# A decode step on one core: the two feed-forward weights loaded behind the last keys and values, the second one in two pieces

## The chip, the core and the metric

One NeuronCore of a Trainium2 chip. The metric is device time in microseconds (us), lower is better. A time is the median of several executions; a profile is one execution, and its time axis begins at the first instruction.

Names used all through: every load of keys (K) or values (V) is 3,072 KB, except that the last head ends in three smaller pieces of 1,920, 768 and 384 KB, K0, K1, K2 and V0, V1, V2. The load before them is the last full K or V. PE is TensorE, PEld its weight loads, DVE VectorE, ACT ScalarE, SP the sync engine. A *row* is one contiguous piece that one of the 16 DMA engines moves (the prediction calls it a packet); a load *lands* when all 16 have done their rows of it. The *clock* is the share of PE's full clock that was granted; PE is *warm* at 1.00.

## The reference, cut to what matters

```python
x = A_x                                    # one token, D = 640
q = layernorm(x) @ wq                      # 32 heads of 192
p = softmax(q . k_cache * 192 ** -0.5)     # 32,768 cached positions a head
h = x + (p . v_cache) @ wo                 # 805 MB of keys and values in all
h2 = h + relu(layernorm(h) @ w1) @ w2      # w1 640 x 1536, w2 1536 x 640
```

The result is `h2`, in bfloat16. The two weights of the last line are 1,920 KB each, 0.5% of the bytes.

## The kernel before

One loop over chunks `g`; each works on a part of a K load. PE transposes blocks of K, multiplies the values of the chunk *before* (`pv(g - 1)`), then multiplies the transposed keys by the query; VectorE does the scores of the other rows. So `pv(g - 1)` stands behind the transposes of chunk `g` in PE's order.

```python
kpool, vpool = ...(bufs=3), ...(bufs=3)          # three buffers for K, three for V
for g in range(G):
    ...
    if end == 0 and c0 == 0:                     # the first chunk of K0
        load_w("w1", B_w1, kpool, "kt", [(0, P)])
        load_w("w2", B_w2, vpool, "vt", [(0, P)])
        for i in range(NEND):                    # NEND = 3
            load_k(ld + i)
        for i in range(NEND):
            load_v(ld + i)
    elif end < 0 and c0 == 0 and g > 0:
        load_k(ld); load_v(ld)
    ...
    transposes(g)
    if g > 0:
        pv(g - 1)
    scores_pe(g)
    sc = scores_dve(g)
    ...
    exp_dve(g, sc)
# ... softmax denominator, last pv, projection, layer norm
for f in range(FT):                              # h1 = relu(hn @ w1), 12 x 5 matmuls
    for c in range(DT): ...
for n in range(DT):                              # y = h1 @ w2, 5 x 12 matmuls
    for f in range(FT):
        nc.tensor.matmul(yps[:, n:n + 1], lhsT=w_t["w2", f][...], rhs=h1T[:, f:f + 1],
                         start=(f == 0), stop=(f == FT - 1))
```

All loads are issued by the sync engine (SP), in the order of the program. The weights use the K and V buffers, so a load of them waits until an older K or V has been used up.

The softmax here doesn't subtract the row's maximum and nothing guards it: scores larger than these inputs give would overflow.

## Time and profile before

| what | number | from |
|---|---|---|
| time | 1963.55 us (1963.5 to 1964.76, 4 runs) | timing |
| profiled span | 1962.3 us | page |
| sync engine's queue, share of the DMA engines | 98.5% | page |
| read from HBM | 825 MB, 420 GB/s over the span | page |
| from K0's first transpose to the end | 28.7 us | timeline |

The kernel is bound by its stream of transfers until about its last 50 us (the DMA share is 0.99 at 1905 to 1910 and 0.49 at 1912 to 1917); there the question is what the compute waits for. The view of waits for the stretch from 1905 to 1945 us (columns: us in total, times, longest us) says it in two lines:

```profile
DVE pr L265 <- DMA kt<-in_A_k_cache_dram: 15.7, 2, 11.5
PE tp L238 <- DMA kt<-in_A_k_cache_dram: 12.6, 2, 9.4
```

Each engine waits twice, for the last full K and for K0, and the longer wait, 9.4 us for PE and 11.5 for VectorE, is the one for K0. The lines of timeline, issues and DMA share for the same stretch stand in the prediction.

### The profile page before, as it was taken

Reading aid. Unit: us, or ns where it says so; the run is one execution under the profiler, and the core shown is the slowest. Engines: PE = TensorE matmul, PEld = TensorE weight load, DVE = VectorE, ACT = ScalarE, POOL = GpSimd, SP = SyncE. Lnnn points to the kernel's source line nnn. Section 1 sums busy time; section 2 is a strip of 40 time slices with the busy share of each in tenths; the row PEclk is TensorE's granted clock in tenths of the full one; section 3 lists DMA queues with packets and bytes.
Section 4 is the critical chain, followed back from the end, with each engine's and each line's share of the span. In section 5 each row is a group of like instructions: output and inputs, shape, how many; then the busy total and the mean of one; then the engine's idle time right before and its main releaser. Section 6 shows DMA issues by size and latency. Waiting matters only on the chain.

```text
span 1962.3 us, 44905 instructions
## 1 busy us (share of the span) xinstructions
PE 1588.3 (81%) x20392; PEld 1116.2 (57%) x20392; DVE 1338.0 (68%) x654; ACT 1067.8 (54%) x2223; POOL 0.7 (0%) x6
## 2 busy tenths in 40 slices
PE   5887888888878788887888788887887878787876
PEld 4555555555556556565555555555555555555554
DVE  5766776667666676776777666766766767677664
ACT  4555555555555555555555555555555545555553
POOL 0000000000000000000000000000000000000000
PEclk9988899989998998988998988988989889999997
DMA  9999999999999999999999999999999999999994
GB/s 405 430 430 431 430 427 430 429 431 430 431 430 428 431 429 430 431 428 431 430 431 430 428 431 428 432 430 423 430 428 429 427 423 430 430 430 426 430 398 187
DMA packets 51506, 827.85 MB, mean 422 GB/s; under 512 B 4596, under 2 KB 17396, under 8 KB 18548
## 3 DMA queue, kind: packets, MB, share of 16 engines
q1 hardware_dynamic: 51316, 824.99, 98.5%
q8 instruction: 159, 2.61, 0.5%
q14 instruction: 31, 0.25, 0.0%
HBM read 824.97 MB, written 0.00 MB: 420 GB/s over the span
## 4 chain that ended last, share of the span: by engine, by line
DMA 78%; PE 16%; ACT 4%; DVE 2%; issue 1%; SPq 0%; ACTq 0%
DMA kt<-in_A_k_cache_dram 78%; PE o_ps L292 7%; PE tp L238 6%; ACT kT L239 3%; DVE pr L265 1%; PE sp L248 1%; PE sp L252 1%; PE sp L250 1%; ACT pB L255 0%; PE qps L204 0%; ACT pA L275 0%; DVE o_pair L313 0%; ACT row_e L207 0%; PE den L298 0%; PE attT L336 0%
## 5 line engine op out<-in xcount | busy, mean ns | idle before, releaser
L239 ACT COPY kT<-tp 128x1024 bf16<-128x1024 bf16 (+1 forms) x1025 | 905.2, 966 | 356.2 <-PE tp L238 353.2
L265 DVE TENSOR_TENSOR pr<-kt,qb 128x2304 f32<-128x2304 bf16 (+1 forms) x258 | 655.0, 2539 | 490.7 <-DMA kt<-in_A_k_cache_dram 487.2
L238 PE MATMUL tp<-ident_b,kt 128*128 128x128 bf16 x7677 | 593.1, 241 | 359.2 <-DMA kt<-in_A_k_cache_dram 283.8
L238 PEld LDWEIGHTS <-kt 128*128 128x128 bf16 x7677 | 524.8, 109 | 398.0 <-DMA kt<-in_A_k_cache_dram 294.6
L268 DVE TENSOR_REDUCE sc<-pr 128x12 f32<-128x2304 f32 (+1 forms) x258 | 654.3, 2536 | 27.6 <-ACT kT L239 1.4
L292 PE MATMUL o_ps<-vt,pB 128*2 128x384 bf16 x2559 | 498.6, 345 | 2.6 <-DMA vt<-in_A_v_cache_dram 2.6
L292 PEld LDWEIGHTS <-pB 128*2 128x2 bf16 x2559 | 203.6, 87 | 226.5 <-issue 65.0
L255 ACT ACTIVATE pB<-sp 128x20 bf16<-128x20 f32 (+1 forms) x258 | 48.5, 188 | 489.2 <-PE sp L252 489.2
L292 PE MATMUL o_ps<-vt,pA 128*2 128x384 bf16 x1537 | 291.9, 326 | 0.0
L248 PEld LDWEIGHTS <-kT 128*128 128x128 bf16 x2559 | 196.0, 96 | 85.8 <-issue 84.4
L248 PE MATMUL sp<-qm,kT 128*128 128x2 bf16 x2559 | 218.5, 164 | 0.5 <-ACT kT L239 0.5
L250 PE MATMUL sp<-qm,kT 128*128 128x1 bf16 x2559 | 214.9, 163 | 0.0
L252 PE MATMUL sp<-qm,kT 128*128 128x1 bf16 x2559 | 214.9, 163 | 0.0
L250 PEld LDWEIGHTS <-kT 128*128 128x128 bf16 x2559 | 198.6, 96 | 0.0
L292 PEld LDWEIGHTS <-pA 128*2 128x2 bf16 x1537 | 129.2, 84 | 120.9 <-issue 0.4
L252 PEld LDWEIGHTS <-kT 128*128 128x128 bf16 x2559 | 197.4, 96 | 0.0
L275 ACT ACTIVATE pA<-sc 128x12 bf16<-128x12 f32 (+1 forms) x258 | 52.9, 205 | 0.0
L255 ACT ACTIVATION_READ_ACCUMULATOR pB<-sp 128x1 f32 x258 | 50.2, 195 | 0.0
L275 ACT ACTIVATION_READ_ACCUMULATOR pA<-sc 128x1 f32 x258 | 49.4, 191 | 0.0
L304 DVE TENSOR_REDUCE rec<-den 128x1 f32<-128x20 f32 x32 | 5.7, 179 | 62.7 <-PE den L298 62.7
L314 ACT ACTIVATE o_pair<-o_ps,rec 2x192 f32<-2x192 f32 x32 | 13.2, 412 | 26.9 <-DVE o_pair L313 26.9
L326 PE MATMUL oT_ps<-ident_f,o_pair 2*128 2x1 f32 x192 | 24.2, 247 | 0.1
(60 smaller groups left out, 192.0 us busy)
## 6 DMA issues: line engine op xcount, KB each, us to landing
kt<-in_A_k_cache_dram SPq DMA_DIRECT2D x127, 3072.0 KB, 35.7
vt<-in_A_v_cache_dram SPq DMA_DIRECT2D x127, 3072.0 KB, 31.4
wq<-in_A_wq_dram SPq DMA_DIRECT2D x8, 960.0 KB, 34.7
wo<-in_A_wo_dram SPq DMA_DIRECT2D x16, 480.0 KB, 31.5
kt<-in_B_w_dram SPq DMA_DIRECT2D x1, 1920.0 KB
vt<-in_B_w_dram SPq DMA_DIRECT2D x1, 1920.0 KB
kt<-in_A_k_cache_dram SPq DMA_DIRECT2D x1, 1920.0 KB, 28.6
vt<-in_A_v_cache_dram SPq DMA_DIRECT2D x1, 1920.0 KB, 17.6
```

The costliest lines, as they stand in the source:

```text
L238: nc.tensor.transpose(out=tp[:, b, :], in_=kt[:, off:off + P], identity=ident_b[:])
L239: nc.scalar.copy(out=kT[:, b0:b0 + nb, :], in_=tp[:, 0:nb, :])
L248: nc.tensor.matmul(sp[:, 2 * i:2 * i + 2], lhsT=kT[:, 3 * i + 1, :], rhs=qm[:, 1:3], start=True, stop=False, skip_group_check=True)
L250: nc.tensor.matmul(sp[:, 2 * i:2 * i + 1], lhsT=kT[:, 3 * i, :], rhs=qm[:, 0:1], start=False, stop=False, skip_group_check=True)
L252: nc.tensor.matmul(sp[:, 2 * i + 1:2 * i + 2], lhsT=kT[:, 3 * i + 2, :], rhs=qm[:, 3:4], start=False, stop=True, skip_group_check=True)
L255: nc.scalar.activation(out=pB[:, 0:JP], in_=sp[:, 0:JP], func=F.Exp, scale=SCALE, accum_out=dsums[:, h, 2 * c + 1:2 * c + 2])
L265: nc.vector.tensor_tensor(out=pr[:, 0:JD, :], in0=kt[:, c0 * Dh:(c0 + JD) * Dh].rearrange("p (j d) -> p j d", d=Dh), in1=qb[:].unsqueeze(1 ...
L268: nc.vector.reduce_sum(out=sc[:, 0:JD], in_=pr[:, 0:JD, :], axis=mybir.AxisListType.X)
L275: nc.scalar.activation(out=pA[:, 0:JD], in_=sc[:, 0:JD], func=F.Exp, scale=SCALE, accum_out=dsums[:, h, 2 * c:2 * c + 1])
L292: nc.tensor.matmul(o[:], lhsT=p, rhs=vt[:, (c0 + j) * Dh:(c0 + j + 2) * Dh], start=first, stop=last)
L314: nc.scalar.activation(out=dst[:, 1, n0:n0 + Dh], in_=o[:, Dh:2 * Dh], func=F.Copy, scale=s[0:2, 1:2])
L326: nc.tensor.matmul(ps[:, b:b + 1], lhsT=src[:, i, b * P:(b + 1) * P], rhs=ident_f[0:2, i:i + 1], start=(i == 0), stop=(i == 1))
```

## The change

The intent: K0 should not queue behind 3.9 MB that are needed only at the very end, and the weights should travel while the compute behind the last values runs. The second product is ordered by rows of w2, so that it could begin on the first piece.

```diff
-    def load_w(name, src, pool, tag, rows):
+    def load_w(name, src, pool, tag, pieces):
...
-        for r0, r1 in rows:
-            nc.sync.dma_start(out=v[r0:r1], in_=...[r0:r1])
+        for i in range(pieces):
+            c0, c1 = i * n // pieces, (i + 1) * n // pieces
+            nc.sync.dma_start(out=v[:, c0:c1], in_=...[:, c0:c1])
...
             if end == 0 and c0 == 0:
-                load_w("w1", B_w1, kpool, "kt", [(0, P)])
-                load_w("w2", B_w2, vpool, "vt", [(0, P)])
                 for i in range(NEND):
                     load_k(ld + i)
                 for i in range(NEND):
                     load_v(ld + i)
+                load_w("w1", B_w1, kpool, "kt", 1)
+                load_w("w2", B_w2, vpool, "vt", 2)
...
-        for n in range(DT):
-            for f in range(FT):
+        for f in range(FT):
+            for n in range(DT):
                 nc.tensor.matmul(yps[:, n:n + 1], ...,
-                                 start=(f == 0), stop=(f == FT - 1))
+                                 start=(f == 0 and n == 0), stop=(f == FT - 1 and n == DT - 1),
+                                 skip_group_check=True)
```

More of the change, by code (lines that the diff above doesn't have):

```diff
@@ L132 @@
     w_t = {}
-    def load_w(name, src, pool, tag, rows):
+    def load_w(name, src, pool, tag, pieces):
         n, N = src.shape[0] // P, src.shape[1]
-        assert n * N <= JL * Dh
+        assert n * N <= JL * Dh and n % pieces == 0
         t = pool.tile([P, JL * Dh], bf16, tag=tag, name=tag)
         v = t[:, 0:n * N].rearrange("p (c n) -> p c n", n=N)
-        for r0, r1 in rows:
-            nc.sync.dma_start(out=v[r0:r1], in_=src.rearrange("(c p) n -> p c n", p=P)[r0:r1])
+        for i in range(pieces):
+            c0, c1 = i * n // pieces, (i + 1) * n // pieces
+            nc.sync.dma_start(out=v[:, c0:c1], in_=src.rearrange("(c p) n -> p c n", p=P)[:, c0:c1])
         for c in range(n):
```

## The prediction

> **What bounds the kernel now.** I read the page first, for the row of DMA shares and the chain that ended last; then the DMA issues, the timeline and the busy time by stretch of the last 70 us. The page:
>
> ```profile
> DMA  9999999999999999999999999999999999999994
> DMA 78%; PE 16%; ACT 4%; DVE 2%; issue 1%; SPq 0%; ACTq 0%
> ```
>
> The first line is the busy share of the 16 DMA engines in 40 slices: full until the last slice (49 us). The second is the chain: 78% transfers. So for some 1,900 us the kernel streams K and V at about 430 GB/s. The change removes no byte, so that part stays. What can move is the end: work that begins only when the last keys land. The timeline of PE, then the sync engine's DMA issues (start, us, engine, line, what):
>
> ```profile
> 1918.38 1.50 PE L238 MATMUL tp<-ident_b,kt 128*128 128x128 bf16 x24
> 1920.57 1.79 PE L292 MATMUL o_ps<-vt,pB 128*2 128x384 bf16 x10
> 1922.19 1.14 PE L292 MATMUL o_ps<-vt,pA 128*2 128x384 bf16 x6
> 1933.61 2.10 PE L238 MATMUL tp<-ident_b,kt 128*128 128x128 bf16 x18 [9.45 <-DMA kt<-in_A_k_cache_dram]
> 1935.64 3.32 PE L292 MATMUL o_ps<-vt,pB 128*2 128x384 bf16 x10
> 1938.80 1.14 PE L292 MATMUL o_ps<-vt,pA 128*2 128x384 bf16 x6
> 1940.33 1.17 PE L238 MATMUL tp<-ident_b,kt 128*128 128x128 bf16 x18
> 1941.43 1.14 PE L292 MATMUL o_ps<-vt,pB 128*2 128x384 bf16 x6
> ...
> 1955.61 1.74 PE L394 MATMUL h1ps<-xn_ln,kt 128*128 128x1 bf16 x60 [1.36 <-DVE xn_ln L186]
> 1957.62 1.74 PE L401 MATMUL yps<-h1T,vt 128*128 128x1 bf16 x60 [0.27 <-ACT h1T L397]
> ```
> ```profile
> 1893.83 0.38 SPq L140 DMA_DIRECT2D kt<-in_B_w_dram  x1
> 1902.00 0.38 SPq L140 DMA_DIRECT2D vt<-in_B_w_dram  x1
> 1904.96 18.24 SPq L123 DMA_DIRECT2D kt<-in_A_k_cache_dram  x3
> 1923.25 17.53 SPq L123 DMA_DIRECT2D vt<-in_A_v_cache_dram  x3
> ```
>
> See three things. PE stands still 9.45 us for the ending keys (call the three ending pieces K0, K1, K2 and V0, V1, V2; the full-size load ahead of them is "the last full K, V"). From K0 at 1933.6 to the span's end at 1962.3 nothing waits for a transfer: it is pure compute, 28.7 us. And w1, w2 are issued ahead of K0. The busy time by stretch tells how they travel (the last two columns are DMA share and GB/s):
>
> ```profile
> 1905.00:1910.00 5.00, 3.45 (x46) 1.99 (x44) 2.52 (x1) 2.38 (x7) 0.00 (x0) 1.00 0.99 391
> 1912.00:1917.00 5.00, 5.00 (x42) 3.82 (x40) 4.86 (x3) 3.55 (x4) 0.00 (x0) 0.71 0.49 205
> 1918.00:1921.00 3.00, 2.74 (x54) 2.33 (x52) 2.90 (x2) 2.39 (x7) 0.00 (x0) 1.00 0.55 205
> 1923.00:1926.00 3.00, 1.16 (x33) 0.81 (x30) 0.00 (x0) 0.47 (x4) 0.00 (x0) 1.00 1.02 393
> 1929.00:1933.00 4.00, 0.00 (x0) 0.00 (x0) 0.00 (x0) 0.00 (x0) 0.00 (x0) 0.50 1.01 430
> 1935.00:1939.00 4.00, 4.00 (x19) 1.79 (x18) 3.86 (x3) 1.94 (x3) 0.00 (x0) 0.53 0.51 217
> ```
>
> From 1912 to 1921 and again from 1935 to 1939 the share is half. The packet records say who works: packets of 3,072 bytes (w1's rows; K2 and V2 have them too, but are not yet issued) appear from 1899 to 1905 and again from 1917 to 1922; of 1,280 bytes (w2 here) from 1904 to 1911 and again from 1922 to 1928. So one half of the engines, the leading one, runs some 18 us ahead of the other, the lagging one, and every load lands when the laggards have done their half. The laggards never rest until 1940: they end the last full V at 1917.3, w1 at 1922, w2 at 1928.3, and then reach K0. The leaders starve because K0's issue takes until 1920.
>
> **What the Trainium skill says.** "DMA: Bandwidth & Descriptors", section "Queues, rings and completion order": "On each SDMA engine descriptors are consumed in ring order". The trace agrees: K0 is 1,920 KB, 4.6 us at 430 GB/s, yet it landed 28.6 us after its issue, behind the weights. Same page, "Why a DMA increments its semaphore by 16 and not by 1": the engines of a DMA finish independently, and only the full count means that all has landed. The half shares above agree: the slower half decides. "TensorE: Matmul & The Clock Gate", "What's actually happening": after an idle window of about 3.4 us the array falls to half clock. It agrees: granted clock 0.50 at 1929 to 1933, and the 18 transposes then took 2.10 us against 1.17 for 18 warm ones. "PSUM — Partial Sum Buffer", "The four PSUM rules": two groups open at once in one bank cannot both clear the written bits; hence the changed product has one start and one stop for all five columns. No run yet shows that; the attention projection (L336) already uses this form.
>
> **The change part by part.** Instruction order: the sync engine's queue alone is reordered (one DMA more); every other engine has as many instructions as before.
>
> (a) *K0 no longer waits for w1 and w2 on the lagging engines.* K0 moves up two places in the issue order, as it now takes the key buffer that w1 took (issue near 1893.8); K1 takes the one K0 took (1905), V0 the one w2 took. On the lagging half nothing lies between the last full V (done at 1917.3) and K0. A K0 packet of 15,360 bytes took 0.573 us, 8 per engine: 4.6 us. K0 lands at about 1922.3 instead of 1933.6: 11 us earlier.
>
> (b) *PE cannot use all of it.* It ends the scores of the preceding chunk only at 1924.1. So K0's transposes start there: 1933.6 - 1924.1 = 9.5 us won, which is the whole idle time.
>
> (c) *PE stays warm.* 18 transposes: chain step 1.03 us instead of 2.10. The 16 value matmuls behind them: 2.77 us (1920.57 to 1923.33) instead of 4.3. Won: 1.07 + 1.5 = 2.5 us. The next transposes start at about 1924.1 + 1.03 + 2.8 + 0.55 (scores) = 1928.5, where they were at 1940.4.
>
> (d) *V0 may now be a little late.* Lagging half: K0 until 1922, K1 (8 x 0.234 us) 1924, K2 (8 x 0.121) 1925, V0 (4.6) 1929.6, landing about 1930. Its first matmul could start at 1929.5. Cost: 0.5 us. V1 (1931.6 on the ring) and V2 (1932.6) are wanted at 1935.6 and 1938: in time.
>
> (e) *The weights come last, behind compute.* w1: 40 packets an engine of 0.121 us, 4.8 us, until 1937.4; w2: 96 of 0.055 us, 5.3 us, pieces done at 1940 and 1942.7, landed by 1944 or so. Wanted: from the first V0 matmul to the first feed-forward product it was 1955.61 - 1941.43 = 14.1 us; from 1930.0 that makes w1's product start at 1944.1, the w2 product 2.0 us later, its second half 3 us later. w1 has 6 us to spare, w2's second piece 3 us.
>
> Their buffers: w1 takes the last full K's (read until 1920.6), w2 the last full V's (its matmuls end at 1928). Both issues come before the lagging engines are ready for them (1932.6, 1937.4).
>
> (f) *Reordering the second product*: 60 matmuls before and after, 1.75 us either way. The split in two: one more DMA. Both worth about 0.
>
> Sum: -9.5 - 2.5 + 0.5 = **-11.5 us**: span 1962.3 - 11.5 = 1950.8; the timed median is 1.2 us above the profiled span (1963.51 against 1962.3), so **1952.0 us**, 0.6% faster.
>
> **Rivals.** *Hidden anyway:* the bytes are the same and DMA is at its limit, so time stays at 1963.5. For it: 98.5% DMA share over the span. Against it: 28.7 us at the end have almost no transfers in their second half, so weights put there fill a hole. *Bytes only:* 3.93 MB at 430 GB/s is 9.1 us, so 1954.4; this misses the clock, and that the laggards take 11 us for them. *A new wait for the weights:* if the issue of w1 or w2 is held up (K0's took 15 us behind w2), or the laggards are further behind than I think, PE waits at the first or second feed-forward product; w2 landing 4 us later than in (e) would cost about 1 us, 8 us about 5, so 1953 to 1957. Against it: the K and V pieces ahead need only 8 descriptors an engine each, where w2 needs 96. *Values late:* V1 waits in the queue for a values buffer; it becomes free near 1918, well before it is needed, but if this slips by 15 us, it costs some 3 us.
>
> **Range and chances.** A gain below 9 us needs one of the last two rivals; above 13 us there is nothing left to take, since PE is then busy or in a chain of dependent steps. The runs of before lie within 1.3 us. So 1948.5 to 1957.5. A 2% change is 39 us, more than the whole tail: within 2% is nearly sure.
>
> **What would show it.** In the changed profile: no PE wait of more than 1 us for keys after 1915; K0's transposes at about 1924 at full clock; the DMA share half or full but not zero until about 1943; the h1ps matmuls at about 1944, released by xn_ln (the layer norm) and not by a DMA; the yps matmuls without a gap in their middle; the 60 yps matmuls in 1.75 us. Wrong would be a wait of PE for in_B_w ahead of h1ps or yps, or in the middle of yps (step e); a wait of the values matmuls for V1 or V2 (step d); K0 landing later than 1926 (step a).

## The result, and the profile after

The changed kernel takes **1954.31 us** (1954.08 to 1954.44, 4 runs) against 1963.55. Ratios here are the mean time of one kernel's runs over that of the other's of the same rounds, so not quite the ratio of the medians: 0.9951, 95% interval 0.9934 to 0.9969. That is 0.5% faster, within the 2% that count as the same, and 2.3 us above the predicted 1952.0. The profiled span fell by 10.0 us, to 1952.3.

The page of the changed kernel, the same two lines as before (DMA share in 40 slices; the chain that ended last):

```profile
DMA  9999999999999999999999999999999999999996
DMA 77%; PE 17%; ACT 4%; DVE 1%; issue 1%; SPq 0%; ACTq 0%
```

Only the last slice differs: the engines are busy for 0.6 of it instead of 0.4. The stream itself is as it was. Next the DMA issues of the changed kernel's sync engine:

```profile
1893.43 12.61 SPq L123 DMA_DIRECT2D kt<-in_A_k_cache_dram  x3
1906.10 13.78 SPq L123 DMA_DIRECT2D vt<-in_A_v_cache_dram  x3
1922.03 0.38 SPq L141 DMA_DIRECT2D kt<-in_B_w_dram  x1
1929.27 4.31 SPq L141 DMA_DIRECT2D vt<-in_B_w_dram  x2
```

K0 is issued at 1893.43, where w1 was; the long stretches of the first two rows are gaps between the three issues, in which the next piece waits for its buffer. Then PE (L239 transposes, L293 value matmuls, L395 and L402 the two feed-forward products):

```profile
1912.12 3.38 PE L239 MATMUL tp<-ident_b,kt 128*128 128x128 bf16 x30 [3.39 <-DMA kt<-in_A_k_cache_dram]
...
1919.74 1.50 PE L239 MATMUL tp<-ident_b,kt 128*128 128x128 bf16 x24
...
1925.38 1.16 PE L239 MATMUL tp<-ident_b,kt 128*128 128x128 bf16 x18
1926.48 1.79 PE L293 MATMUL o_ps<-vt,pB 128*2 128x384 bf16 x10
...
1929.64 1.17 PE L239 MATMUL tp<-ident_b,kt 128*128 128x128 bf16 x18
1931.56 1.14 PE L293 MATMUL o_ps<-vt,pB 128*2 128x384 bf16 x6 [0.76 <-DMA vt<-in_A_v_cache_dram]
...
1945.51 1.74 PE L395 MATMUL h1ps<-xn_ln,kt 128*128 128x1 bf16 x60 [1.36 <-DVE xn_ln L187]
1947.52 1.74 PE L402 MATMUL yps<-h1T,vt 128*128 128x1 bf16 x60 [0.27 <-ACT h1T L398]
```

K0's transposes at 1925.38 carry no wait: the 9.45 us are gone, and PE comes to them from other work. What is left is 0.76 us for V0 at 1931.56. Neither feed-forward product waits for a transfer. The first matmul on V0 moved from 1941.43 to 1931.56, by 9.9 us, and from there to the end both kernels take 20.8 to 20.9 us. The busy time by stretch in the changed kernel (last two columns: DMA share, GB/s):

```profile
1912.00:1917.00 5.00, 4.88 (x36) 3.72 (x37) 4.72 (x2) 3.55 (x4) 0.00 (x0) 0.50 0.74 316
1918.00:1921.00 3.00, 3.00 (x60) 2.37 (x58) 2.90 (x2) 1.03 (x5) 0.00 (x0) 1.00 0.69 222
1935.00:1939.00 4.00, 3.97 (x44) 2.10 (x42) 1.27 (x2) 2.47 (x7) 0.00 (x0) 1.00 0.88 321
1941.00:1944.00 3.00, 2.06 (x27) 1.87 (x27) 0.65 (x6) 1.70 (x2) 0.00 (x0) 1.00 0.38 141
```

From 1935 the engines carry the weights (0.88, then 0.38 as the leading half is done), beside PE's work on the last chunks. The column before them is the granted clock: 0.50 at 1912 to 1917, where it was 0.71 before; this was not in the prediction's account. It comes with PE's wait of 3.39 us for the last full K, but not as the idle window of about 3.4 us that the prediction quotes from the Trainium skill's page on TensorE would have it: PE stood still from 1908.73, and the trace has the clock at half from 1910.36, 1.6 us into that wait. For the 9.45 us wait of the kernel before the window does fit; for this one the measurement decides.

### The profile page after: what moved, and what is told of

Same layout as the page of the kernel before. It is cut to its first block, busy times and chain, and to the rows that moved or that the text cites. A ratio compares the mean times of both kernels' runs of the same rounds, so it can differ in the third digit from the quotient of the medians.

```text
span 1952.3 us, 44906 instructions
## 1 busy us (share of the span) xinstructions
PE 1594.4 (82%) x20392; PEld 1122.4 (57%) x20392; DVE 1338.0 (69%) x654; ACT 1067.5 (55%) x2223; POOL 0.7 (0%) x6
## 4 chain that ended last, share of the span: by engine, by line
DMA 77%; PE 17%; ACT 4%; DVE 1%; issue 1%; SPq 0%; ACTq 0%
DMA kt<-in_A_k_cache_dram 75%; PE o_ps L293 8%; PE tp L239 6%; ACT kT L240 3%; DMA vt<-in_A_v_cache_dram 1%; DVE pr L266 1%; PE sp L249 1%; PE sp L253 1%; PE sp L251 1%; PE qps L205 0%; ACT pA L276 0%; ACT pB L256 0%; DVE o_pair L314 0%; PE oT_ps L327 0%; ACT row_e L208 0%
## 5 line engine op out<-in xcount | busy, mean ns | idle before, releaser
L239 PE MATMUL tp<-ident_b,kt 128*128 128x128 bf16 x7677 | 599.3, 242 | 342.8 <-DMA kt<-in_A_k_cache_dram 269.7
L239 PEld LDWEIGHTS <-kt 128*128 128x128 bf16 x7677 | 531.1, 110 | 381.2 <-DMA kt<-in_A_k_cache_dram 280.2
L293 PE MATMUL o_ps<-vt,pB 128*2 128x384 bf16 x2559 | 498.8, 346 | 2.6 <-DMA vt<-in_A_v_cache_dram 2.6
L293 PEld LDWEIGHTS <-pB 128*2 128x2 bf16 x2559 | 203.8, 87 | 226.9 <-issue 65.9
L293 PE MATMUL o_ps<-vt,pA 128*2 128x384 bf16 x1537 | 291.9, 326 | 0.0
L293 PEld LDWEIGHTS <-pA 128*2 128x2 bf16 x1537 | 129.1, 84 | 120.8
L315 ACT ACTIVATE o_pair<-o_ps,rec 2x192 f32<-2x192 f32 x32 | 13.2, 412 | 26.9 <-DVE o_pair L314 26.9
## 6 DMA issues: line engine op xcount, KB each, us to landing
vt<-in_A_v_cache_dram SPq DMA_DIRECT2D x1, 1920.0 KB, 25.4
```

The costliest lines, as they stand in the source:

```text
L239: nc.tensor.transpose(out=tp[:, b, :], in_=kt[:, off:off + P], identity=ident_b[:])
L293: nc.tensor.matmul(o[:], lhsT=p, rhs=vt[:, (c0 + j) * Dh:(c0 + j + 2) * Dh], start=first, stop=last)
L315: nc.scalar.activation(out=dst[:, 1, n0:n0 + Dh], in_=o[:, Dh:2 * Dh], func=F.Copy, scale=s[0:2, 1:2])
```

## The experiments

Four theories were set against each other. *The lagging half* (the prediction): only the time that the slower DMA engines spend on what stands in front of K0 and V0 counts. *The split*: the pieces of w2 carry part of the gain. *The held-up issue*: the many short rows of w2 blocked K0's issue, the leading engines starved, and that was the loss. *Weights not hidden*: they cost time at the end of the changed kernel.

An interval of such a ratio is about 0.0013 to each side, 2.5 us. So differences of 1 us are read from run ranges that don't overlap and from the traces, and are called open where neither tells.

**The loads alone, and the split alone** (before: 1964.65). The first keeps the new place of the loads, with one piece and the old product order; the second keeps the old place, with two pieces and the new order.

```diff
# order_only, against the changed kernel
-                load_w("w2", B_w2, vpool, "vt", 2)
+                load_w("w2", B_w2, vpool, "vt", 1)       # and the product's loops as before
# split_only: both load_w lines ahead of load_k, the rest as changed
```

> Both weights are the last loads as in the changed kernel, but w2 in one piece and the second product in the order of before. Main theory (the position of the loads is all; the laggard half of the DMA engines reaches K0 sooner): within 0.5 us of the changed kernel, 1953.8 to 1954.8, since the last piece of w2 ended near 1944 in the changed kernel's trace and its product starts only at 1947.5. Rival (the split carries part of the gain by letting the product start on the first piece): 1955 or more, with PE waiting for in_B_w ahead of the second product.

> Weights in front of K0 as before, but w2 in two pieces and the product ordered by piece. Main theory: as before, 1963.0 to 1964.0. Rival (split or order is worth something by itself): 1 us or more below 1963.5.

Measured: the loads alone 1954.37 (ratio 0.9949), the split alone 1964.34 (0.9998, interval 0.9986 to 1.0011). The whole gain is the place of the loads. The split is worth nothing that these runs can see, as the second product wasn't waiting for w2 in any of them.

**One weight at a time**.

```diff
# w1_last: w2 ahead of load_k, w1 behind load_v.   w2_last: the other way round
```

> w2 in front of K0 (two pieces), w1 behind V2. Main theory (what counts is the time that the lagging half spends on the rows in front of K0): w2 takes 96 rows an engine of 0.055 us, 5.3 us, so K0 lands 5 us later than in the changed kernel, near 1929.5; PE, free at 1925.4, waits 4 us and may fall to half clock: 1958 to 1960.5. Rival (the loss of before came from K0's issue being held up by the many short rows of w2, which starved the leading half): almost nothing won, 1962 to 1963.5.

> w1 in front of K0, w2 behind V2. Main theory: w1 takes 40 rows an engine of 0.121 us, 4.8 us, K0 lands near 1929: 1957.5 to 1960. Rival (held-up issue by w2's short rows): with w2 away the issue runs free and nearly the whole gain is had, 1954.5 to 1955.5.

Measured: 1959.54 with only w1 moved, 1959.45 with only w2 moved: half the gain each (5.1 and 5.2 us of 10.3). K0's transposes on PE, in the run with w1 moved and then in the run with w2 moved:

```profile
1929.01 2.10 PE L239 MATMUL tp<-ident_b,kt 128*128 128x128 bf16 x18 [3.56 <-DMA kt<-in_A_k_cache_dram]
```
```profile
1929.67 2.10 PE L239 MATMUL tp<-ident_b,kt 128*128 128x128 bf16 x18 [4.53 <-DMA kt<-in_A_k_cache_dram]
```

In the changed kernel VectorE started on K0 at 1924.21, the moment it landed (PE was still busy); here K0 lands 4.8 and 5.5 us later. That each weight costs the same, though one has 40 rows an engine and the other 96, speaks for time on the engines and against the held-up issue, which asked for 1962 or more in the first run and about 1955 in the second. (The second profile is of that run's slowest execution, 1960.44 us, in which the lagging engines ended the last full V 0.7 us later than in the changed kernel.)

**All bytes in front, in long rows** (before: 1964.15). The weights are read so that a partition's row is one piece of 15,360 bytes. Its output is wrong, which doesn't matter for the time.

```diff
# and both load_w lines ahead of load_k, w2 in one piece
-            nc.sync.dma_start(out=v[:, c0:c1], in_=src.rearrange("(c p) n -> p c n", p=P)[:, c0:c1])
+            nc.sync.dma_start(out=v[:, c0:c1], in_=src.rearrange("(p c) n -> p c n", p=P)[:, c0:c1])
```

> Wrong result on purpose: weights in front of K0 with all their bytes, but read in another order, so that each partition's row is one piece of 15,360 bytes instead of 5 of 3,072 or 12 of 1,280. K0's issue then can't be held up by many rows and the leading half doesn't starve. Main theory (only the time of the lagging half counts): 16 rows of 0.573 us, 9.2 us, instead of 10.1, so about 1 us below before, which was 1964.65 on the chip of the last call: 1963 to 1964.2. Rival (held-up issue and the starved half cost time): 4 us or more below before.

Measured: 1963.37 (1962.75 to 1963.88), ratio 0.9996. Here is K0's issue before, then in this run, each from its timeline of the sync engine, and K0's transposes in this run:

```profile
1904.96 15.16 SPq L123 DMA_DIRECT2D kt<-in_A_k_cache_dram  x1
```
```profile
1905.09 0.33 SPq L123 DMA_DIRECT2D kt<-in_A_k_cache_dram  x1
```
```profile
1933.16 2.10 PE L239 MATMUL tp<-ident_b,kt 128*128 128x128 bf16 x18 [8.67 <-DMA kt<-in_A_k_cache_dram]
```

The hold-up is real: the issue took 15.16 us and now takes 0.33. But K0 lands at 1933.16 instead of 1933.61. By the packet records the leading engines had ended K0's rows at 1915.9 in this run and began them only at 1920.8 in the kernel before, and nothing came of it. This is the clearest test of the lagging half: the held-up issue falls. The Trainium skill's "Perfetto Trace Analysis", section "DMA Instruction — HWDGE (DVE, Sync)", explains how to read the 15.16 us: the profiled time of an issue is that of waiting for and using the descriptor generator, and not the data's. This agrees, since K0's own data needed about 5 us.

**Hardly any weights** (wrong result). One fifth of w1 and one twelfth of w2 in front of K0, nothing behind V2.

```diff
-        for i in range(pieces): ...
+        nc.sync.dma_start(out=v[:, 0:1], in_=src.rearrange("(c p) n -> p c n", p=P)[:, 0:1])
         for c in range(n):
-            w_t[name, c] = v[:, c, :]
+            w_t[name, c] = v[:, 0, :]
```

> Wrong result on purpose: in front of K0 only one twelfth of w2 and one fifth of w1 are loaded (557 KB instead of 3,932), and used for all products; nothing behind V2. Main theory (in the changed kernel the weights are wholly hidden, what is left is K0, V0 and a chain of compute): 8 rows of 0.121 and 8 of 0.055 us an engine, 1.4 us, stand in front of K0 and V0, so 1.0 to 1.6 us over the changed kernel, 1955.3 to 1956. Rival (the weights still cost time at the end of the changed kernel): 1954 or less, since they are nearly gone.

Measured: 1956.34 (1955.44 to 1958.0), not below the changed kernel but above it. So weights that are nearly absent gain nothing over weights loaded last: they are hidden. The time is a little above what was expected; V0 came at 1932.8 as foreseen, but after the wait of 1.95 us for it PE was at half clock for a spell (the next 15 transposes took 1.75 us instead of 1.00). The run also answers a rival that was not listed: in the changed kernel K0 is not only first in the queue but issued 11.5 us sooner (1893.43 against 1904.96). Here it was issued at 1905.10 and landed at 1925.44, so most of the gain does not need the sooner issue.

**More bytes behind V2**. Half of w2 twice more, ahead of w1 and of w2, into unused ends of their buffers.

```diff
+        x = t[:, n * N:n * N + 6 * D].rearrange("p (c n) -> p c n", n=D)
+        nc.sync.dma_start(out=x, in_=B_w2.rearrange("(c p) n -> p c n", p=P)[:, 0:6])
```

> The changed kernel with 1,920 KB more (half of w2 twice over, into unused ends of the buffers) behind V2 and ahead of w1 and of w2. Main theory: the lagging half takes 2 x 48 rows of 0.055 us, 5.3 us more, so the last piece lands near 1949.2 where it ended near 1943.9; it is wanted at 1948.4 (the middle of the second product), so 0.8 to 2 us over the changed kernel, 1955 to 1956.3, with PE waiting for in_B_w in the second product alone. Rival (no slack: the loads at the end set the end): 5 us more, 1959. Rival (slack larger than 6 us): no change.

Measured: 1955.71 (1955.3 to 1957.34). The two products on PE:

```profile
1946.50 1.74 PE L396 MATMUL h1ps<-xn_ln,kt 128*128 128x1 bf16 x60 [1.36 <-DVE xn_ln L189]
1948.51 1.90 PE L403 MATMUL yps<-h1T,vt 128*128 128x1 bf16 x60 [0.27 <-ACT h1T L399]
```

The time is within the expected range, but not for the expected reason: the second product is stretched by 0.16 us alone (1.90 against 1.74), in one gap ahead of its 31st matmul, the first on the second piece of w2. The other 1.0 us lies ahead of the first product and comes with a clock of 0.62 at 1941 to 1944. So the slack of the changed kernel is about what this load takes, some 5 us; the time itself settles nothing, as the changed kernel run again gave 1955.66.

**V0 ahead of K1 and K2**, a version to beat the changed kernel.

```diff
-                for i in range(NEND): load_k(ld + i)
-                for i in range(NEND): load_v(ld + i)
+                load_k(ld);     load_v(ld)
+                load_k(ld + 1); load_k(ld + 2)
+                load_v(ld + 1); load_v(ld + 2)
```

> The changed kernel with the last values' order K0, V0, K1, K2, V1, V2. Main theory: in the changed kernel PE waited 0.76 us for V0, behind K1 and K2 (2.9 us on the lagging half); now V0 lands before it is wanted and PE runs through: 0.5 to 1 us below the changed kernel, 1953.3 to 1954. Rival (K1 now comes late instead, or the wait moves to the buffers): no change, or slower.

Measured: 1953.20 (1951.82 to 1953.57), ratio to before 0.9943, and correct. All its runs lie below all nine timed runs of the changed kernel. They were run at other times. In its timeline the first matmul on V0 follows its transposes at once, at 1929.63, with no wait.

**The clock** (before: 1964.05). The changed kernel again, for the same rounds; then V0 early, with 50 transposes of the identity in PE's wait for the last full K; then the kernel *before*, with 140 of them in its wait for K0.

```diff
+            if end == -1 and c0 == 0:            # before_warm: end == 0, 140 times
+                wm = mm_bank([P, P], bf16, "wm")
+                for _ in range(50):
+                    nc.tensor.transpose(out=wm[:], in_=ident_b[:], identity=ident_b[:])
             transposes(g)
```

> The changed kernel itself again, to have it in the same rounds as the next ones. 1954 to 1955 with before at 1963.5 to 1964.7.

> V0 early as in the last call, and 50 transposes of the identity into an unused PSUM tile, ahead of the first transposes of the last full K, where PE stands still for 3.1 us and then works at half clock. They should take about 2.8 us (50 x 0.056) of that wait. Theory (after the last full K has landed the chain is PE's own work, and in v0_early 0.6 us of its 30 transposes and 0.9 us of the 10 value matmuls behind them come from the half clock): 1.0 to 1.6 us below v0_early, which was 1953.2: 1951.6 to 1952.3. Rival (V0 or the lagging half's next piece then becomes the wait): 0 to 0.5 us.

> The kernel before, with 140 transposes of the identity ahead of K0's transposes, so that PE works through most of its 9.45 us wait for K0 (140 x 0.056 = 7.8 us) and keeps its clock. Tests step c alone: 1.07 us of transposes and 1.5 us of value matmuls, 2 to 2.6 us below before: 1961 to 1962.5. Rival (the clock is worth nothing since something else sets the pace, the evacuations or the values): within 0.5 us of before.

Measured: changed again 1955.66 (1954.15 to 1955.71), ratio 0.9955; V0 early and warm 1952.36 (1952.18 to 1952.96), 0.9942; before and warm 1963.53 (1963.41 to 1964.13), 0.9998. The middle one is clear of the changed kernel in the same rounds, by some 3 us; that the extra transposes help beyond V0's place is not shown: it is 0.8 us across two calls, the trace has a new wait of 0.95 us for K0, and the first matmul on V0 starts at 1929.77, no sooner than the 1929.63 without them. The profile's shorter span (1950.6 against 1951.0) comes from later on, where the clock is 0.87 instead of 0.67 at 1938 to 1944. The third result was a miss, and the most useful run of all. PE in it:

```profile
1924.54 7.98 PE L365 MATMUL wm<-ident_b 128*128 128x128 bf16 x140
1933.68 1.18 PE L238 MATMUL tp<-ident_b,kt 128*128 128x128 bf16 x18 [1.17 <-DMA kt<-in_A_k_cache_dram]
1934.79 1.79 PE L292 MATMUL o_ps<-vt,pB 128*2 128x384 bf16 x10
...
1937.95 1.17 PE L238 MATMUL tp<-ident_b,kt 128*128 128x128 bf16 x18
1941.05 1.14 PE L292 MATMUL o_ps<-vt,pB 128*2 128x384 bf16 x6 [1.93 <-DMA vt<-in_A_v_cache_dram]
```

The clock did its work: 18 transposes in 1.18 us instead of 2.10, 10 value matmuls in 1.79 instead of 3.32. Then PE stood 1.93 us for V0, which landed at 1941.0, where the kernel before had arrived at 1941.4. In the kernel before, a slow PE and a late V0 came together at the same point; taking one away left the other.

**Clock and V0 together, weights in front** (before: 1963.95), to test that reading.

```diff
# before_warm, with load_k(ld); load_v(ld) first, then K1, K2, V1, V2
```

> The kernel before, weights in front, with the 140 transposes that keep PE's clock up, and V0 loaded ahead of K1 and K2. Corrected theory (both kernels end a fixed chain of compute after V0 lands or PE is through with the work ahead of it, whichever is later; in before the two came together, V0 at 1941.0 and PE at 1941.4, so a warm clock alone only brought a wait of 1.93 us for V0): V0 now lands 2 to 3 us sooner and that wait goes, 1.7 to 2.3 us below before_warm, which was 1963.53 with before at 1964.05: 1961.2 to 1962.2, with no PE wait for in_A_v_cache. Rival (the clock brings nothing, whatever V0 does): 1963 to 1964.

Measured: 1961.80 (1961.58 to 1962.53), ratio 0.9990 (0.9977 to 1.0004), as the corrected theory said, with no wait for values; the first matmul on V0 starts at 1939.19 instead of 1941.05. The interval reaches 1, but the runs of before (1963.3 to 1964.94) don't overlap with these. So the warm clock with V0 early is 2.15 us below before; the warm clock alone was 0.5 us, which is within the noise. V0 early without the clock, weights in front, was not run.

## Why the prediction was right or wrong

The direction, the order of size and the mechanism held: the prediction's range contains 1954.31. The gain was over-stated by 2.3 us. By its steps:

- **(a) K0 sooner: right in kind, mis-sized.** It said 1922.3; VectorE started on K0 at 1924.21, so K0 moved by 9.4 us and not 11. The term that failed is "done at 1917.3": by the packet records the eight lagging engines ended the last full V between 1916.9 and 1918.7, so 1917.3 holds for some of them, and a load lands with its slowest engine. From 1918.7 the weights' rows take until 1928.7, close to the 10.1 us of the row times, and K0 lands 4.9 us later. In the changed kernel the last full V ended at 1919.0, 1.7 us after the predicted time, and K0 landed 5.2 us later.
- **(b) The 9.5 us of idle PE: gone, as said.** But PE did not come free at 1924.1. Its chunk of the last full K started 0.5 us later than before (1912.12 against 1911.61), and half clock lasted longer: the 30 transposes took 3.38 us in both kernels, but the 10 value matmuls behind them 2.63 us instead of 1.79. K0's transposes began at 1925.38.
- **(c) The clock, 2.5 us: the transposes and value matmuls got as short as said, but this was not a gain of its own.** The run of before with a warm clock won 0.5 us by the medians, within the noise, and 0.4 us at the first matmul on V0, because V0's landing at 1941.0 stood right behind. The step assumed that PE alone set the pace there.
- **(d) V0 late, 0.5 us: right in kind.** It landed at 1931.5 instead of 1930, and PE waited 0.76 us. The chain of the changed kernel that ended last runs through V0's landing: 9.5 us earlier than the 1941.0 of before. Add the 0.4 us that PE was later than V0 in before, and there are the 9.9 us by which everything after moved.
- **(e) The weights hidden: right.** The last row of w2 ended at 1943.7 (said: 1942.7), its product began at 1947.5. Hardly any weights were no faster, and 1,920 KB more stretched the product by 0.16 us.
- **(f) Split and new order worth 0: right** (split alone 0.9998).
- **The timed median** was taken as span plus 1.2 us; the same execution gives span plus 1.8. That is 0.6 us of the 2.3; the later V0 is most of the rest.

Of the rivals, "bytes only" (1954.4) named the number almost exactly. It got there because the gain is the travel time of the weights ahead of K0 and V0, 9.4 us against its 9.1, with the clock alone adding almost nothing. What it doesn't have is which engines count: the long-rows run freed the leading half for K0 and won no more than 0.8 us by the medians, not clear of the noise.

What stays open: what V0 early is worth in the kernel before without the warm clock; what decides whether a short wait of PE costs it the clock; why one half of the DMA engines runs behind the other, and whether it is worth anything to bring them together.

## What to carry to other kernels

In a kernel bound by its stream, look at what the last dependent piece queues behind: everything that is needed later than that piece belongs behind it, as long as the compute that follows is longer than its transfer. Before adding the savings of two waits on one chain, ask what lands next: a wait removed shows the next one, and only the latest of them counts. And where a load is spread over many engines, take its landing from the slowest one, not from the first that is done.

## What the Trainium skill lacked or had wrong

- "DMA: Bandwidth & Descriptors", "Why a DMA increments its semaphore by 16 and not by 1", says that engines of one DMA finish independently, but the page does not say how far apart they may run in a plain stream: in the kernel before, the 16 engines ended the last full V up to 19.8 us apart (the first at 1898.9, the last at 1918.7, eight of them from 1916.9 on), and the share of all 16 was 0.49 while the half worked alone.
- The same page's "Specifications" give 512 bytes as the least transfer for full rate. Rows of 1,280 bytes took 0.055 us, 23.3 GB/s an engine; 3,072 bytes 0.121 us, 25.4; 24,576 bytes 0.912 us, 26.9. So 1,280 bytes were still 14% below the longest rows; elsewhere the page names a fixed cost per packet, but no measured rate for rows of these sizes on this chip.
- "Perfetto Trace Analysis", "DMA Instruction — HWDGE (DVE, Sync)", shows a descriptor buffer that fills, but no size and no sign of how long an issue may be held: 15.16 us here behind loads of 40 and 96 rows an engine, 0.33 us behind loads of 8 and 8.
- "TensorE: Matmul & The Clock Gate", "What's actually happening", puts the fall to half clock after an idle window of about 3.4 us, and doesn't say how little work within a window is enough. Here the clock was at half from 1.6 us into a wait of PE (changed kernel) and after one of 1.95 us (hardly any weights), but not after one of 1.93 us (before, warm).
- Not lacking, but confirmed: one start for a bank with five open columns ("PSUM — Partial Sum Buffer", "The four PSUM rules") gave a correct result in the changed kernel and in each run with its product order whose weights were loaded whole and in their order.
